# The last segment's projections are moved into attention's unit 0, between its score steps

## The chip, the cores and the metric

One NeuronCore of a Trainium2 chip runs the whole program. The engines are TensorE (PE; its weight loads are listed as PEld), VectorE (DVE), ScalarE (ACT), GpSimd (POOL) and SyncE (SP, whose queue issues most of the DMAs). The metric is the device time of one execution in microseconds (us), from the first to the last instruction and what lies around them. Less is better.

## The reference, cut to what matters

A transformer block: a layer norm modulated by a condition, attention over 2048 tokens in four segments of 512 with a memory that is carried from segment to segment, and a gated feed-forward layer. Width 576, 32 heads of 18, hidden width 4608, everything fp32.

```python
mod = (silu(c) @ w_mod).reshape(1, 6, 1, -1)
sa, ca, ga, sb, cb, gb = (mod[:, i] for i in range(6))
h = layernorm(x) * (1 + ca) + sa
q, k, v = h @ wq, h @ wk, h @ wv            # 32 heads x 18, 4 segments of 512
M, z = 0, 0
for s in range(4):
    p = softmax(q[s] @ k[s].T * scale + mask)
    a_dot = p @ v[s]
    a_mem = (phi(q[s]) @ M) / (phi(q[s]) @ z + 1e-6)      # phi(t) = t + 1 if t > 0 else exp(t)
    o[s] = g * a_mem + (1 - g) * a_dot
    M, z = M + phi(k[s]).T @ v[s], z + phi(k[s]).sum()
x = x + ga * (o @ wo)
h = layernorm(x) * (1 + cb) + sb
x = x + gb * ((silu(h @ w_gate) * (h @ w_up)) @ w_down)
```

## The kernel before

**Precision.** Matmuls take operands in the form float32r. To keep fp32 accuracy each operand is split into a high and a low part, and a product is made of three matmuls: high by high, high by low, low by high. The width 576 is four blocks of 128 and a rest of 64 (whose two parts share one tile, `hr`, so it needs two matmuls). One output tile of 128 rows by 512 tokens therefore takes 4 x 3 + 2 = 14 matmuls.

**Phase 1, projections.** The loop `for s in range(NSEG)` (L571) goes through the four segments. In this phase the Tile scheduler chooses the order on each engine by data, program order and its own costs. Per segment:

- nine projection tiles (`proj`, L505): five hold K, the last of them half, and the rest Q. Each takes the 14 matmuls of `mm14` (L100) into a PSUM tile `pp` (three buffers). ACT copies `pp` twice, to `fh` (the high part, L513) and `pf` (L514). DVE makes the low part `fl = pf - fh` (L515). SP stores both to DRAM (`kD`, `qD`), from where attention loads them as stacks. For Q rows of segments after the first, DVE makes `min(pf, 0)`, ACT its exponential and DVE `max(pf, 0)` plus that, which is phi(q) (`pq`, L529 to L531), and SP stores it (`qF`, L532).
- `phi_k` (L484 to L488): PE transposes a K tile to `ptk`, ACT and DVE make phi(k) of it (`pe`, `pk`). `ptk` has two buffers.
- four v pieces (`vproj`, `pv`, L545), the transposes of the next segment's input (`trans_in`, `pt`) and the memory update (`mem`, `pm`). Segment 3 has none of these: its v pieces are made in attention.

Two generators are stepped along with it. `early()` makes a part of the score passes of attention's first two units. `late_mod()` works off 20 pieces of `w_mod`: SP loads a piece (`wml`, four buffers, L430), DVE multiplies and adds it to `macc` (L349, L352), and after each fifth piece PE sums `macc` over partitions (`pc`, L359, L362) and DVE stores the sums (`colm`, L365, L366). It takes one step per projection tile from the middle of segment 1, and its last pieces fall into the v pieces of segment 2.

**Phase 2, attention.** From here the order is written by hand (`tc.manual_schedule()`), so each engine runs its instructions in the order of the code. A unit is four heads of one segment, so there are 32 units, eight per segment. Unit u does two passes of scores: the first pass of unit u+2 (matmuls of L184 into `s`, then DVE's custom instruction `junk`, `mx` of L199, which finds the row maxima) and the second pass of unit u (L656 into `s`, then ACT's exponential into `Pt`, L662). It multiplies `Pt` of unit u-1 by v (`av`, L679), transposes the result back (`px`, L700) and combines it. Units 0 to 7 also make the eight v pieces of segment 3 (`pw`, L803). Table `PAT` holds, for eleven slots of a unit, which of these events come in which order: an `a` is a pair of score steps, `M` and `X` are the parts of a v piece, `V` is `av`. Units 1 and 3 run the same row of `PAT`, and units 0 and 2 another.

**Loads of the units.** Four sets of stacks (`ks`, `qs`, for K and Q) are used in turn; `load_unit` (L168) has SP load a unit's four stacks from `kD` and `qD`. Those of units 0 to 2 are loaded in phase 1. Unit 3's set lies in the pool `sk2`, and its loads come first in phase 2, before unit 0. The loads of unit u+3 are issued at the start of unit u. Also ahead of unit 0, SP loads segment 0's v (`vq`, L724).

**Phase 3, feed-forward**, is set by PE and is not touched.

Of the kernel before, what the change touches and what calls it, by code (L numbers as in the profile page):

```python
# [11 lines left out]
ALU = mybir.AluOpType  # L12
# [52 lines left out]
LNA = 1  # L65
# [4 lines left out]
def f32(ap):  # L70
    return ap.bitcast(F32)
# [3 lines left out]
def block(ctx: ExitStack, tc: tile.TileContext, x, wqk, wv, wo, beta, wgu, wd, c, w_mod, wm01, out):  # L75
# [12 lines left out]
    def run(g):  # L88
        for _ in g:
            pass  # L90

    def mm14(ps, wh, wl, xh, xl, xr):
        k = 0
        for kt in range(5):
            if kt < 4:
                pairs = [(wh(kt), xh(kt)), (wl(kt), xh(kt)), (wh(kt), xl(kt))]
            else:
                pairs = [(wh(4), xr()), (wl(4), xr())]
            for a, b in pairs:
                nc.tensor.matmul(ps, lhsT=a, rhs=b, start=(k == 0), stop=(k == 13))  # L100
                k += 1

# [162 lines left out]

    p2, p2r, p7 = ExitStack(), ExitStack(), ExitStack()
    yx2 = pool(p7, "yx2", side="right")
# [5 lines left out]
    def v_ops(s, i, h):  # L273
# [6 lines left out]
        return ops + [(hr[:, tk], wvh[:, 4, sl]), (hr[:, tk], wvl[:, 4, sl])]  # L280

    with ExitStack() as p1:
        wq1 = pool(p1, "wq1")
        raw = pool(p1, "raw1", 2)
# [26 lines left out]

        wqkh = wq1.tile([P, 9, 5, P], F32R, tag="wqkh", name="wqkh")
        wqkl = wq1.tile([P, 9, 5, P], F32R, tag="wqkl", name="wqkl")
        bdm = w1.tile([P, 5, 8, VW], F32, tag="bdm", name="bdm")
# [190 lines left out]
        def proj(s, t):  # L505
            hh, hl, hr = hT[s]
            pp = ps.tile([P, L], F32, tag="p", name="pp", bufs=3)
            mm14(pp, lambda k: wqkh[:, t, k, :], lambda k: wqkl[:, t, k, :], lambda k: hh[k],
                 lambda k: hl[k], lambda: hr)
# [4 lines left out]
            nc.scalar.copy(f, pp)  # L514
            nc.vector.tensor_tensor(fl, f, f32(fh), op=ALU.subtract)  # L515
            k0, k1 = 128 * t, min(128 * t + 128, D)
            if k0 < D:
                n = k1 - k0
                nc.sync.dma_start(kD[s][k0:k1, 0:2, :], f32(fh[:n]).unsqueeze(1).to_broadcast([n, 2, L]))
                nc.sync.dma_start(kD[s][k0:k1, 2, :], f32(fl[:n]))  # L520
            q0, q1 = max(128 * t - D, 0), 128 * t + 128 - D
            if q1 > 0:
                n = q1 - q0
                r = P - n
                nc.sync.dma_start(qD[s][q0:q1, 0:3:2, :], f32(fh[r:]).unsqueeze(1).to_broadcast([n, 2, L]))
                nc.sync.dma_start(qD[s][q0:q1, 1, :], f32(fl[r:]))
                if s > 0:
                    e = pb.tile([P, L], F32, tag="pq1", name="pq1")
                    nc.vector.tensor_scalar(e[r:], f[r:], 0.0, None, op0=ALU.min)  # L529
                    nc.scalar.activation(e[r:], e[r:], AF.Exp)  # L530
                    nc.vector.scalar_tensor_tensor(e[r:], f[r:], 0.0, e[r:], op0=ALU.max, op1=ALU.add)  # L531
                    nc.sync.dma_start(qF[s][q0:q1, :], e[r:])  # L532
            return f
# [36 lines left out]

        for s in range(NSEG):  # L571
            gens = []
            if s == 0:
                gens.append(load_wv())
            if s + 1 < NSEG:
                gens.append(prep(s + 1))
            g = chain(*gens)
# [6 lines left out]
            for t in QKORD:  # L584
                if s == 0 and t + 3 < 9:
                    split_qk(t + 3)
                if s == 0 and t + 4 < 9:
                    load_qk(t + 4)
                f = proj(s, t)
                if pend is not None:  # L590
                    phi_k(s, *pend)
                    pend = None
                if t < 5 and s < 3:
# [9 lines left out]
            tg = trans_in(s + 1) if s + 1 < NSEG else iter(())  # L603
            for i in range(4):
                if i == 3:
                    for _ in g:
                        pass
                if s < 3:
                    vproj(s, i)
                next(g, None)  # L610
# [7 lines left out]
            next(tg, None)  # L618
            if s < 3:
                for _ in mem(s):  # L620
                    next(tg, None)
            for _ in tg:
# [7 lines left out]
    wk = pool(p2, "wk2", 2)  # L630
    opl_ = pool(p2, "op2")
    ps = pool(p2, "ps2", 2, space=PSUM)
# [92 lines left out]

    w3 = pool(p2r, "w3", side="right")
    o3 = pool(p2r, "o3", 2, side="right")
    yt = {}

    def yh(k, kb):  # L730
        return yt[1][:, k - 1, kb] if k else yt[0][kb]

    woh = w3.tile([P, 5, D], F32R, tag="woh", name="woh")
    wol = w3.tile([P, 5, D], F32R, tag="wol", name="wol")

# [50 lines left out]
    def wo_x(s, i, h):  # L786
# [3 lines left out]
        if h == 1:  # L790
            (nc.scalar if (s, i) == (2, 3) else nc.sync).dma_start(xD[s][:, i, :], xr)

    vst3 = {}
# [114 lines left out]
    def event(ev, u):  # L908
        n, a = ev[0], ev[1:]
        s, q = divmod(u, 8)  # L910
        if n == "V":
            for j in a:
# [11 lines left out]
        elif n == "d":  # L924
            comb_b(u - 1)
        elif n == "f" and s < 3 and q < 4:
            phi_q(s + 1, q + 1)
        elif n == "h" and s < 3 and q == 0:
            phi_q(s + 1, 0)
# [17 lines left out]
        elif n in "MX":  # L947
            w = u - 9
            if u < 8:
                if n == "M":  # L950
# [484 lines left out]
    with tc.manual_schedule():  # L1435
        new_stack(3, sk2)
        load_unit(3)
        for j in range(4):
            load_v(0, j)
        ot[0] = opl_.tile([P, 4, D], F32, tag="o0", name="o0")  # L1440
        for u in range(NU + 1):
            s, q = divmod(u, 8)
            if u:
                load_unit(u + 3)
            ma, mb = [], []
# [290 lines left out]
```

## Time and profile before

| what | us |
|---|---|
| three timed runs | 1858.72, 1859.91, 1860.71 (median 1859.91) |
| the profiled execution, its own time | 1856.97 |
| its span, first to last instruction | 1855.2 |
| segment 2: projections | 138.15 to 169.04 |
| segment 2: v pieces | 169.04 to 185.69 |
| transposes for segment 3 and memory update | 185.69 to 193.51 |
| segment 3: projections | 193.51 to 222.90 |
| unit 0 | 222.90 to 238.65 |
| unit 1 | 238.65 to 250.41 |
| unit 2 | 250.41 to 261.02 |
| unit 3 | 261.02 to 270.57 |

The stages are bounded by the first instruction on PE that belongs to the next one (in the last of the transposes, two matmuls of segment 3's first tile already stand between them). A row of the profile gives for one engine the start, the duration, the line, the operation with the tile that it writes and those that it reads, and in brackets how long the engine was idle before it and what ended that. In a table by windows, the columns are the length, the busy time of the five engines with the number of instructions, the clock that TensorE was granted as a share of full speed, the mean busy share of the DMA engines, and GB/s.

### The profile page before, as it was taken

The page shows a single profiled execution, that of the slowest core. Times are in us where ns is not written, and L with a number is a line of the kernel's source. Part 1 is how long each engine was busy: PE and PEld are TensorE (multiplying, and loading weights), DVE is VectorE, ACT ScalarE, POOL GpSimd, SP SyncE. Part 2 cuts the span into 40 slices and gives each one's busy share as a digit, 9 for nine tenths or more (in the row PEclk, how much of TensorE's full clock was granted, in tenths as well). Part 3 has the DMA queues.
Part 4 walks back from the last instruction along what each step waited for, and adds up shares of the span by engine and source line. Part 5 has one row for each costly group of instructions (what it writes and reads, how often), then busy time and mean ns, then how long its engine had stood idle before and what let it go on. Part 6 is the DMA issues. An engine that isn't in the chain of part 4 may idle for free.

```text
span 1855.2 us, 31128 instructions
## 1 busy us (share of the span) xinstructions
PE 1816.8 (98%) x11061; PEld 1518.0 (82%) x11061; DVE 1492.6 (80%) x3309; ACT 958.2 (52%) x2137; POOL 495.8 (27%) x702
## 2 busy tenths in 40 slices
PE   8999989999999999999999999999999999999999
PEld 5888756666667888888888888888888888888888
DVE  7566468888886888888888888758888888888887
ACT  6344457667776545445445444434454544544441
POOL 2010036454563345545544544300000000000000
PEclk9999999999999999999999999999999999999999
DMA  8677565558658654555555444395332333334331
GB/s 298 224 242 253 212 175 154 152 149 217 177 149 278 218 185 157 172 194 176 166 183 168 132 137 167 125 297 172 127 105 85 120 105 107 100 102 127 104 100 52
DMA packets 178562, 304.49 MB, mean 164 GB/s; under 512 B 25304, under 2 KB 108184, under 8 KB 176616
## 3 DMA queue, kind: packets, MB, share of 16 engines
q1 hardware_dynamic: 151032, 248.66, 42.7%
q10 hardware_dynamic: 27376, 53.86, 8.2%
q8 instruction: 87, 1.43, 0.3%
q14 instruction: 67, 0.55, 0.1%
HBM read 188.42 MB, written 113.33 MB: 163 GB/s over the span
## 4 chain that ended last, share of the span: by engine, by line
PE 87%; DVE 6%; DMA 4%; issue 1%; ACT 1%; SPq 1%; POOL 0%; ACTq 0%; DVEq 0%; POOLq 0%
PE A L1273 24%; PE pd L1401 13%; PE C L1273 12%; PE pd L1382 10%; PE B L1273 6%; PE pp L100 5%; PE av L679 3%; PE pw L784 3%; PE pv L545 2%; DVE junk L199 2%; PE s L184 2%; PE s L656 2%; DMA qs<-qD 1%; PE pn L862 1%; DMA y<-yD 1%
## 5 line engine op out<-in xcount | busy, mean ns | idle before, releaser
L1273 PE MATMUL A<-y,wh 128*128 128x512 f32 x1152 | 406.1, 393 | 1.1 <-ACT B L1319 0.7
L199 DVE CUSTOM_DVE_ANT_0 junk<-s,tri 128x384 bf16<-128x384 f32 (+3 forms) x512 | 222.0, 486 | 45.8 <-PE s L184 27.2
L1238 DVE TENSOR_TENSOR wl<-O,wh 128x256 fp32r<-128x256 f32 x504 | 253.7, 509 | 2.1 <-ACT wh L1237 1.6
L1273 PEld LDWEIGHTS A<-y,wh 128*128 128x128 f32 x1152 | 216.6, 188 | 45.9 <-ACT B L1319 2.2
L1273 PE MATMUL A<-y,wl 128*128 128x512 f32 x576 | 226.8, 394 | 0.0
L1387 DVE TENSOR_TENSOR acc<-acc,pd 128x576 f32<-128x576 f32 x216 | 162.3, 752 | 59.4 <-PE pd L1382 51.5
L1273 PE MATMUL C<-y,wh 128*128 128x512 f32 x576 | 202.9, 393 | 1.1 <-DVE cu L1296 1.1
L662 ACT ACTIVATE Pt<-s 128x512 f32<-128x512 f32 (+2 forms) x384 | 179.1, 525 | 44.7 <-PE s L184 24.4
L1237 ACT CAST wh<-O 128x256 fp32r<-128x256 f32 x504 | 197.5, 405 | 1.7 <-DMA yD<-st 0.8
L1401 PE MATMUL pd<-dh,ah 128*128 128x288 f32 x640 | 188.9, 295 | 0.5 <-DVE x L1405 0.5
L1401 PE MATMUL pd<-dh,al 128*128 128x288 f32 x640 | 189.0, 295 | 0.0
L1401 PE MATMUL pd<-dl,ah 128*128 128x288 f32 x640 | 188.7, 295 | 0.0
L1411 DVE TENSOR_TENSOR acc<-acc,pd 128x576 f32<-128x576 f32 x156 | 117.0, 750 | 87.9 <-PE pd L1401 87.2
L1228 POOL TENSOR_TENSOR O<-O 128x384 f32<-128x384 f32 x132 | 149.6, 1148 | 135.3 <-DMA O<-in_wgu_dram 61.5
L1342 ACT CAST ah<-sg 128x512 fp32r<-128x512 f32 x192 | 119.1, 621 | 77.2 <-DVE sg L1297 70.3
L1343 DVE TENSOR_TENSOR al<-sg,ah 128x512 fp32r<-128x512 f32 x192 | 136.3, 710 | 10.0 <-ACT ah L1342 9.9
L1382 PE MATMUL pd<-dh,ah 128*128 128x288 f32 x448 | 133.0, 297 | 0.0
L1382 PE MATMUL pd<-dh,al 128*128 128x288 f32 x448 | 132.5, 296 | 0.0
L1382 PE MATMUL pd<-dl,ah 128*128 128x288 f32 x448 | 132.3, 295 | 0.0
L184 PE MATMUL s<-ks,qs 54*128 54x512 f32 (+1 forms) x480 | 122.9, 360 | 8.2 <-DVE mx L199 4.2
L656 PE MATMUL s<-qs,ks 56*128 56x256 f32 (+3 forms) x512 | 124.5, 356 | 3.4 <-ACT Pt L662 2.8
L1401 PEld LDWEIGHTS pd<-dh,ah 128*128 128x128 f32 x640 | 120.7, 189 | 6.8 <-DVE x L1405 0.8
(388 smaller groups left out, 4337.2 us busy)
## 6 DMA issues: line engine op xcount, KB each, us to landing
O<-in_wgu_dram SPq DMA_DIRECT2D x36, 768.0 KB
O<-oD SPq DMA_DIRECT2D x36, 512.0 KB
oD<-O ACTq DMA_DIRECT2D x34, 512.0 KB
ks<-kD SPq DMA_DIRECT2D x64, 216.0 KB
qs<-qD SPq DMA_DIRECT2D x64, 216.0 KB
O<-in_wgu_dram SPq DMA_DIRECT2D x36, 384.0 KB
rD<-wr ACTq DMA_DIRECT2D x36, 336.0 KB
wr<-rD SPq DMA_DIRECT2D x35, 336.0 KB
```

The lines of the kernel that those rows point to most:

```text
L184: nc.tensor.matmul(bank[:, n * o:n * o + n], lhsT=qst[b][r, h // 2, 128 * i:128 * i + 128], rhs=kst[b][r, h // 2, 0:n], start=True, stop=True)
L199: nc.vector.tensor_tensor_reduce(junk[:, :n], bank[:, n * o:n * o + n], tri[:, L - n:], 1.0, -3e38, op0=ALU.add, op1=ALU.max, accum_out=mx ...
L656: nc.tensor.matmul(bank[:, n * o:n * o + n], lhsT=kst[u % NB][r, g // 2, 128 * j:128 * j + 128], rhs=qst[u % NB][r, g // 2, 128 * j:L], st ...
L662: nc.scalar.activation(pt[:, hs[0]:hs[-1] + 1:2, :n], bank[:, :n * per].rearrange("p (a b) -> p a b", a=per), AF.Exp, scale=SCALE)
L1228: eng.tensor_tensor(o[:, d], o[:, a], o[:, b], op=op)
L1237: nc.scalar.copy(wh, o)
L1238: later.append(lambda: nc.vector.tensor_tensor(wl, o, f32(wh), op=ALU.subtract))
L1273: nc.tensor.matmul(bank, lhsT=a, rhs=b, start=(first and n == 0), stop=(n == 6), skip_group_check=not first)
L1343: later.append(lambda: nc.vector.tensor_tensor(al, src, f32(ah), op=ALU.subtract))
L1382: nc.tensor.matmul(pd[:, i, :288], lhsT=a[:, tk], rhs=w, start=(k == 0), stop=(k == 2))
L1387: nc.vector.tensor_tensor(o, o, pd[:, :, :288], op=ALU.add)
L1401: nc.tensor.matmul(pd[:, i, :288], lhsT=a[:, tk], rhs=w, start=(k == 0), stop=(k == 5))
```

## The change

Attention's pools are opened right after segment 2, and phase 1's loop ends with it. Segment 3's nine projection tiles are nine events `W0` to `W8` of unit 0, four steps each, with three pairs of score steps after some of them; `W9` is the v piece that unit 0 had before. A tile's PSUM buffer is now one of the two of tag `x`. Its copies, low part and phi(q) go to two scratch tiles, `tmpa` and `tmpb`, in turn. They are not issued right behind the tile's matmuls: each further `W` step first advances the tiles before it by one part (low part and minimum; exponential and sum; stores). `late_mod` takes two steps per tile instead of one in the first five tiles of segment 2. Segment 0's v is loaded in slots 2 to 5 of unit 0. The weights' pool (`wqkh`, `wqkl`) lives on until the start of unit 1, and the pools of the output projection are opened there.

```diff
@@ PAT
+       ("W0 W0 W0 W0 a a a", "W1 W1 W1 W1 W2 W2 W2 W2 a a a", "W3 W3 W3 W3 W4 W4 W4 W4", "a a a", "W5 W5 W5 W5 W6 W6 W6 W6", "a a a", "W7 W7 W7 W7", "W8 W8 W8 W8", "W9 W9", "W9 W9", "P"))
@@ phase 1
-        for s in range(NSEG):
+        for s in range(3):
...
                 if s > 1 or s == 1 and t > 4:
                     next(gl, None)
+                if s > 1 and t < 5:
+                    next(gl, None)
@@ new, in attention
+    def seg3(t):
+        if not tmp3:
+            a = sk2.tile([P, 5, L], F32, tag="pq", name="tmpa").rearrange("p a b -> p (a b)")
+            b = vp.tile([P, 4, VC], F32, tag="vq", name="tmpb").rearrange("p a b -> p (a b)")
+            for v in (a, b):
+                tmp3.append([v[:, L * i:L * i + L] for i in range(4)])
+        f, fh, fl, e = tmp3[t % 2]
+        fh, fl = fh.bitcast(F32R), fl.bitcast(F32R)
+        pp = ps.tile([P, L], F32, tag="x", name="pp", bufs=XB)
+        ops = p_ops(3, t)
+        for c in range(WC):
+            for n in range(14 * c // WC, 14 * (c + 1) // WC):
+                nc.tensor.matmul(pp, lhsT=ops[n][0], rhs=ops[n][1], start=(n == 0), stop=(n == 13))
+            if c < 3:
+                yield
+        nc.scalar.copy(fh, pp)
+        nc.scalar.copy(f, pp)
+        yield
+        _, q1, r = q_rows(t)
+        nc.vector.tensor_tensor(fl, f, f32(fh), op=ALU.subtract)
+        if q1 > 0:
+            nc.vector.tensor_scalar(e[r:], f[r:], 0.0, None, op0=ALU.min)
+        yield
+        if q1 > 0:
+            nc.scalar.activation(e[r:], e[r:], AF.Exp)
+            nc.vector.scalar_tensor_tensor(e[r:], f[r:], 0.0, e[r:], op0=ALU.max, op1=ALU.add)
+        yield
+        k_store(3, t, fh, fl)
+        q_store(3, t, fh, fl)
...
+            nc.sync.dma_start(qF[3][q0:q1, :], e[r:])
+        yield
+    def seg3_step(t):
+        for g in list(s3q):
+            if next(g, 0) == 0:
+                s3q.remove(g)
...
+        if t == 9:
+            s3[9] = c = s3.get(9, -1) + 1
+            v_m(0, c)
+            if c == 3:
+                v_x(0)
+            return
+        if t not in s3:
+            s3[t] = [seg3(t), 0]
+        s3[t][1] += 1
+        next(s3[t][0])
+        if s3[t][1] == 4:
+            s3q.append(s3[t][0])
@@ phase 2
         load_unit(3)
-        for j in range(4):
-            load_v(0, j)
-        ot[0] = opl_.tile([P, 4, D], F32, tag="o0", name="o0")
...
+            if u == 1:
+                while s3q:
+                    seg3_step(-1)
+                p2q.close()
+                w3 = pool(p2r, "w3", side="right")
...
-                for ev in PAT[q // 4 * 2 + u % 2][k].split():
+                for ev in PAT[q // 4 * 2 + u % 2 if u else 4][k].split():
...
+                elif u == 0 and 2 <= k < 6:
+                    load_v(0, k - 2)
```

`p_ops`, `k_store`, `q_rows` and `q_store` hold what `proj` had in its own body. Two loads of `qF` that stood in units 0 and 1 now come together in unit 1.

PE, from the last matmuls of segment 3's projections into unit 0, before (`pp` is a projection tile, `s` a score tile; the line L656 is the second pass, L184 the first):

```order
L100 MATMUL pp<-hl_2191,wqkh 128x512
L100 MATMUL pp<-hr,wqkh 128x512
L100 MATMUL pp<-hr,wqkl 128x512
L656 MATMUL s_2602<-qs_982,ks_983 128x512
L184 MATMUL s_2605<-ks_991,qs_990 128x512
L184 MATMUL s_2612<-ks_991,qs_990 128x512
L656 MATMUL s_2611<-qs_982,ks_983 128x512
L656 MATMUL s_2618<-qs_982,ks_983 128x512
L184 MATMUL s_2619<-ks_991,qs_990 128x512
L184 MATMUL s_2626<-ks_991,qs_990 128x512
L656 MATMUL s_2625<-qs_982,ks_983 128x512
```

PE at the same place now, in unit 0 behind its first projection tile (L661 and L174 are the two passes, L807 the tile):

```order
L807 MATMUL pp<-hl_2197,wqkh 128x512
L807 MATMUL pp<-hr,wqkh 128x512
L807 MATMUL pp<-hr,wqkl 128x512
L661 MATMUL s_2369<-qs_982,ks_983 128x512
L174 MATMUL s_2372<-ks_991,qs_990 128x512
L174 MATMUL s_2379<-ks_991,qs_990 128x512
L661 MATMUL s_2378<-qs_982,ks_983 128x512
L661 MATMUL s_2385<-qs_982,ks_983 128x512
L174 MATMUL s_2386<-ks_991,qs_990 128x512
L807 MATMUL pp<-hh_2190,wqkh 128x512
L807 MATMUL pp<-hh_2190,wqkl 128x512
```

Before, all twelve pairs of score steps stood behind the ninth tile, with parts of the v piece between them from the seventh on. Now they go by threes, six matmuls or a few more at a time, behind the tiles 0, 2, 4 and 6.

DVE in the projections of segment 2, before, from the normalisation of the next segment's `x` on (`pe`, `pk` are phi(k), `pq` phi(q)):

```order
L249 TENSOR_SCALAR x_1743<-x_1743,mv,rs 128x576 x4
L488 SCALAR_TENSOR_TENSOR pk<-ptk,pe 128x4x128
L515 TENSOR_TENSOR fl<-pf,fh 128x512
L486 TENSOR_SCALAR pe<-ptk 128x512
L515 TENSOR_TENSOR fl<-pf,fh 128x512
L529 TENSOR_SCALAR pq_1900<-pf 64x512
L488 SCALAR_TENSOR_TENSOR pk<-ptk,pe 128x4x128
```

The same place now:

```order
L239 TENSOR_SCALAR x_1743<-x_1743,mv,rs 128x576 x4
L503 SCALAR_TENSOR_TENSOR pk<-ptk,pe 128x4x128
L380 TENSOR_SCALAR colm<-pc 128x2
L381 TENSOR_SCALAR colm<-pc 96x1
L380 TENSOR_SCALAR colm<-pc 128x2
L381 TENSOR_SCALAR colm<-pc 96x1
L364 TENSOR_SCALAR macc<-wml,sg 128x576
L529 TENSOR_TENSOR fl<-pf,fh 128x512
L501 TENSOR_SCALAR pe<-ptk 128x512
L367 SCALAR_TENSOR_TENSOR macc<-wml,sg,macc 128x576
L529 TENSOR_TENSOR fl<-pf,fh 128x512
L503 SCALAR_TENSOR_TENSOR pk<-ptk,pe 128x4x128
```

Four `colm` and two `macc` now stand between the two `pk`, and the minimum of the first `pq` has gone behind the second. On PE the `pc` matmuls that belong to these `colm` stand ahead of the third `ptk`; before they stood behind the fifth.

SP at the end of segment 3's stores, before:

```order
L525 DMA qD_90<-fh 128x2x512
L526 DMA qD_90<-fl 128x512
L532 DMA qF_98<-pq_2547 128x512
L125 DMA ks_2588<-ones 10x8x128
L125 DMA ks_2588<-ones 2x8x128
L168 DMA ks_2588<-kD_91 54x2x512
L168 DMA qs_2587<-qD_87 54x2x512
L168 DMA ks_2588<-kD_91 54x2x512
L168 DMA qs_2587<-qD_87 54x2x512
L724 DMA vq_2595<-vD_99 128x624 x4
```

SP now, at the end of segment 2's stores:

```order
L298 DMA qD_89<-fl 128x512
L539 DMA qF_97<-pq_2083 128x512
L115 DMA ks_2342<-ones 10x8x128
L115 DMA ks_2342<-ones 2x8x128
L158 DMA ks_2342<-kD_91 54x2x512
L158 DMA qs_2341<-qD_87 54x2x512
L158 DMA ks_2342<-kD_91 54x2x512
L158 DMA qs_2341<-qD_87 54x2x512
L287 DMA kD_94<-tmpa 128x2x512
L288 DMA kD_94<-tmpa 128x512
```

And at the end of segment 3's stores, where unit 1 begins:

```order
L297 DMA qD_90<-tmpa 128x2x512
L298 DMA qD_90<-tmpa 128x512
L826 DMA qF_98<-tmpa 128x512
L1033 DMA woraw<-in_wo_dram 128x576
L158 DMA ks_983<-kD_91 54x2x512
L158 DMA qs_982<-qD_87 54x2x512
L158 DMA ks_983<-kD_91 54x2x512
L158 DMA qs_982<-qD_87 54x2x512
```

The six loads of unit 3's stacks have gone from behind all of segment 3's stores to ahead of the first of them. Behind the last store now stand a piece of the output weights and the loads for unit 4. From unit 1 on, every engine runs the same instructions in the same order as before.

More of the change, by code (lines that the diff above doesn't have):

```diff
@@ L90, in run @@
             pass
[L92 to L101, printed above, removed]
     cst = pool(ctx, "cst")
@@ L280, in v_ops, with p_ops, k_store, q_rows @@
         return ops + [(hr[:, tk], wvh[:, 4, sl]), (hr[:, tk], wvl[:, 4, sl])]
+    wq1 = pool(p2q, "wq1", side="right")
+    wqkh = wq1.tile([P, 9, 5, P], F32R, tag="wqkh", name="wqkh")
+    wqkl = wq1.tile([P, 9, 5, P], F32R, tag="wqkl", name="wqkl")
+    def p_ops(s, t):
+        hh, hl, hr = hT[s]
+        ops = []
+        for k in range(4):
+            ops += [(wqkh[:, t, k, :], hh[k]), (wqkl[:, t, k, :], hh[k]), (wqkh[:, t, k, :], hl[k])]
+        return ops + [(wqkh[:, t, 4, :], hr), (wqkl[:, t, 4, :], hr)]
+    def k_store(s, t, fh, fl):
+        k0, k1 = 128 * t, min(128 * t + 128, D)
+        n = k1 - k0
+        if n > 0:
+            nc.sync.dma_start(kD[s][k0:k1, 0:2, :], f32(fh[:n]).unsqueeze(1).to_broadcast([n, 2, L]))
+            nc.sync.dma_start(kD[s][k0:k1, 2, :], f32(fl[:n]))
+    def q_rows(t):
+        q0, q1 = max(128 * t - D, 0), 128 * t + 128 - D
+        return q0, q1, P - (q1 - q0)
+    def q_store(s, t, fh, fl):
+        q0, q1, r = q_rows(t)
+        if q1 > 0:
+            nc.sync.dma_start(qD[s][q0:q1, 0:3:2, :], f32(fh[r:]).unsqueeze(1).to_broadcast([q1 - q0, 2, L]))
+            nc.sync.dma_start(qD[s][q0:q1, 1, :], f32(fl[r:]))
     with ExitStack() as p1:
-        wq1 = pool(p1, "wq1")
         raw = pool(p1, "raw1", 2)
@@ L505, in proj @@
         def proj(s, t):
-            hh, hl, hr = hT[s]
             pp = ps.tile([P, L], F32, tag="p", name="pp", bufs=3)
-            mm14(pp, lambda k: wqkh[:, t, k, :], lambda k: wqkl[:, t, k, :], lambda k: hh[k],
-                 lambda k: hl[k], lambda: hr)
+            for n, (a, b) in enumerate(p_ops(s, t)):
+                nc.tensor.matmul(pp, lhsT=a, rhs=b, start=(n == 0), stop=(n == 13))
             f = pb.tile([P, L], F32, tag="pf", name="pf")
@@ L515, in proj @@
             nc.vector.tensor_tensor(fl, f, f32(fh), op=ALU.subtract)
[L516 to L521, printed above, removed]
+            k_store(s, t, fh, fl)
+            q_store(s, t, fh, fl)
+            q0, q1, r = q_rows(t)
             if q1 > 0:
[L523 to L526, printed above, removed]
                 if s > 0:
@@ L592, in block @@
                     pend = None
-                if t < 5 and s < 3:
+                if t < 5:
                     pend = (t, f)
@@ L618, in block @@
             next(tg, None)
-            if s < 3:
-                for _ in mem(s):
-                    next(tg, None)
+            for _ in mem(s):
+                next(tg, None)
             for _ in tg:
@@ L948, in event @@
             w = u - 9
-            if u < 8:
+            if 0 < u < 8:
                 if n == "M":
```

40 lines of the change are left out of this document (24 added, 16 removed), and 2 rows, old and new, of the table PAT.

## The prediction
> **What bounds the kernel now.** I read the page first: the engines' shares and the chain that ended last.
>
> ```profile
> span 1855.2 us, 31128 instructions
> PE 1816.8 (98%) x11061; PEld 1518.0 (82%) x11061; DVE 1492.6 (80%) x3309; ACT 958.2 (52%) x2137; POOL 495.8 (27%) x702
> PE 87%; DVE 6%; DMA 4%; issue 1%; ACT 1%; SPq 1%; POOL 0%; ACTq 0%; DVEq 0%; POOLq 0%
> ```
>
> TensorE is busy for 98% of the span, so 38.4 us of it are idle in all. An edit that only moves matmuls can gain no more than such idle time, or matmuls that ran at a lower clock. So the next view is the table by stages (front table's bounds).
>
> ```profile
> 138.15:169.04 30.89, 29.45 (x151) 23.62 (x150) 24.40 (x53) 13.85 (x25) 1.83 (x2) 1.00 0.82 282
> 193.51:222.90 29.39, 29.39 (x126) 23.21 (x125) 10.67 (x18) 13.51 (x25) 0.00 (x0) 1.00 0.65 227
> 222.90:238.65 15.75, 9.99 (x48) 6.61 (x48) 8.84 (x36) 8.20 (x17) 3.72 (x10) 0.72 0.74 209
> 238.65:250.41 11.76, 11.51 (x83) 6.48 (x84) 6.29 (x25) 6.15 (x14) 2.90 (x6) 0.80 0.68 216
> 250.41:261.02 10.61, 9.60 (x85) 6.08 (x85) 9.33 (x40) 6.84 (x17) 4.25 (x10) 1.00 0.46 129
> 261.02:270.57 9.55, 9.30 (x84) 5.91 (x84) 6.79 (x32) 6.25 (x14) 2.92 (x9) 1.00 0.54 163
> ```
>
> Segment 3's projections are pure PE time, 29.39 of 29.39 at full clock. Unit 0 behind them is the worst stage here: 5.76 of 15.75 idle, and a clock of 0.72. Unit 1 hardly waits, but runs at 0.80. The waits of PE in unit 0, and then the chain there, say why:
>
> ```profile
> PE s L184 <- DMA qs<-qD: 3.3, 1, 3.3
> PE s L184 <- DVE mx L199: 2.0, 3, 0.9
> PE s L656 <- ACT pf L514: 0.5, 1, 0.5
> ```
>
> ```profile
> 227.08 0.32 SPq L532
> ...
> 229.22 0.42 SPq L168
> ...
> 230.46 8.05 DMA qs<-qD
> ...
> 238.65 0.89 PE s L184 x2
> ```
>
> Score steps alone outrun DVE (2.0). Then unit 0 has no more work, and unit 1's first pass waits 3.3 for unit 3's stacks, whose last load SP issues at 230.46, because it stands behind segment 3's last store (227.08). It takes 8.05 to land. The clock answers to this:
>
> ```profile
> 222.00:226.00 4.00, 2.52 (x13) 1.18 (x11) 2.49 (x6) 3.45 (x7) 0.00 (x0) 1.00 0.88 340
> 228.00:233.00 5.00, 5.00 (x20) 3.90 (x20) 2.28 (x10) 1.36 (x3) 0.30 (x1) 0.50 0.45 140
> 238.60:243.00 4.40, 4.35 (x23) 1.52 (x27) 1.31 (x4) 0.60 (x1) 0.00 (x0) 0.50 0.83 286
> 243.00:245.00 2.00, 2.00 (x24) 1.01 (x16) 0.38 (x1) 1.00 (x2) 1.32 (x1) 0.89 0.61 173
> 152.00:156.00 4.00, 2.56 (x14) 1.95 (x13) 3.94 (x9) 1.80 (x4) 0.00 (x0) 1.00 0.49 166
> ```
>
> After the thin stretch to 226 it is half, and after the wait to 238.65 it is half again until 243. In the last row a thin stretch that stayed at full clock.
>
> **The change, part by part.** All against the profiled execution, 1856.97 (the median of the runs is 2.94 above it).
>
> *Segment 2's projections.* `late_mod` brings DVE five `macc` earlier. Groups of DVE's instructions there, and PE's one stall:
>
> ```profile
> L352 DVE SCALAR_TENSOR_TENSOR macc<-wml,sg,macc 128x576 f32<-128x576 f32 (+1 forms) x11 | 8.9, 814 | 1.5 <-DMA wml<-in_w_mod_dram 1.4
> L515 DVE TENSOR_TENSOR fl<-pf,fh 128x512 fp32r<-128x512 f32 x9 | 6.2, 688 | 4.1 <-ACT pf L514 4.1
> 153.77 0.63 PE ptk L484 x4
> 154.40 3.03 PE pp L100 x13
> 157.42 0.39 PE ptk L484 x4
> 157.81 0.54 PE pc L359 x4
> ```
>
> ```profile
> 153.77 0.63 PE L484 MATMUL ptk<-ident,pf 128*128 128x128 f32 x4 [1.44 <-DVE pk L488]
> 159.15 0.50 PE L100 MATMUL pp<-hh,wqkh 128*128 128x512 f32 x1
> ```
>
> The `pc` matmuls for `colm` cost 159.15 - 157.81 = 1.34 there. They now come before the transpose that waits 1.44, so the 1.44 is filled: a gain of 1.34. But between the two `pk` that release the last two transposes now stand four `colm` and two `macc` (one of them the plain multiplication). Without them the second `pk` is in time, since the transpose at 157.42 does not wait. With them I work out 0.3 + 0.5 + 0.6 + 0.6 + 0.75 + 0.6 + 0.6 = 4.0 (a 688 ns instruction starts 0.60 after the one ahead) from the end of the first `pk`, 153.6, to 157.6, so PE may wait about 0.4 at 157.4. Net 0.9; I take 0.8. Bounds: +1.3 if it waits for nothing. On the other side, DVE has 24.40 of 30.89 busy; with 5 x 0.81 = 4.1 it has 28.5, so it fits, but its queue is in order, and a `macc` that waits for its `wml` holds `fl` and `pk` up. Two pieces per tile of 3.3 us with three loaded ahead leave a load 4.9 us. Its price when late is in these rows:
>
> ```profile
> 133.09 6.28 DMA wml<-in_w_mod_dram
> 148.62 2.67 DMA kD<-fl
> ```
>
> A landing of 2.67 is free. One of 6.28 costs 6.28 - 4.9 = 1.4 each time, and twice it would be a loss of 2.8 - 0.8 = 2.
>
> *Segment 3's projections.* The same 126 matmuls at 0.233, no gain. The two PSUM buffers (three before) are freed by ACT's two copies and the scratch by the stores. What could be late is costed under the second rival. At the seam the first tile no longer fills gaps among the last transposes: it stands behind them, and its thirteenth matmul needs `hr`, made from the last transpose by three instructions of ACT and DVE of about 0.7. Twelve matmuls (2.8) and the memory update cover these 2.1 with the handovers; the cost is nothing to 0.5, and I take 0.
>
> *Unit 0.* With tiles between the groups of scores, DVE and ACT get 3.3 to 6.5 us for the three pairs that PE gives out at a time, so the 2.0 of waits for `mx` go. The 0.5 for `pf` goes, as each tile has another behind it. Unit 3's loads are issued before the first store, some 35 us ahead of their use; the 3.3 goes. What stays is PE time at full clock. Unit 2 runs the same row of the table, with three groups in addition that unit 0 doesn't have:
>
> ```profile
> L679 PE MATMUL av<-Pt,vq 128*32 128x512 f32 (+3 forms) x32 | 2.4, 436 | 0.0
> L700 PE MATMUL px<-ident,avs 128*128 128x128 f32 x4 | 0.6, 272 | 0.0
> L214 PE MATMUL pmt<-ident,mc 128*32 128x128 f32 x1 | 0.3, 284 | 0.0
> ```
>
> 9.60 - 2.4 - 0.6 - 0.3 = 6.3. So 15.75 becomes 6.3: a gain of 9.45, the largest term.
>
> *Unit 1.* It now follows dense work. Unit 3 runs the same row of the table at clock 1.00 in 9.55, against 11.76: a gain of 2.2. The chain shows the same difference in `av`:
>
> ```profile
> 239.84 4.07 PE av L679 x32
> ...
> 262.01 2.29 PE av L679 x32
> ```
>
> [...]
>
> *What is late next.* The last tile's low part, minimum, exponential and sum fall into unit 0's v piece and the head of unit 1. The rows of the kernel before for such steps are 0.69, 0.42, 0.63, 0.69 in the order of a tile:
>
> ```profile
> 220.93 0.69 DVE L515 TENSOR_TENSOR fl<-pf,fh 128x512 fp32r<-128x512 f32 x1 [0.85 <-ACT pf L514]
> 222.00 0.63 ACT L530 ACTIVATE pq<-pq 128x512 f32<-128x512 f32 x1 [1.10 <-DVE pq L529]
> 222.66 0.69 DVE L531 SCALAR_TENSOR_TENSOR pq<-pf,pq 128x512 f32<-128x512 f32 x1 [0.70 <-ACT pq L530]
> ```
>
> Queued behind them are the first `junk` and `Pt` of unit 1, for which PE waits after three pairs; I take 1.0 (0 to 2). SP issues the last `qF` store only when that sum is there, some 2 to 3 us into unit 1, and the piece of output weights and unit 4's four loads stand behind it. They are needed at unit 2's start, 9.55 in; with 8.05 to land they come at 10 to 11. I take 0.5 (0 to 3).
>
> *Sum:* 0.8 + 9.45 + 2.2 - 1.5 = 10.95. The profiled execution would be 1846.0; the median 1859.91 - 10.95 = 1849.0.
>
> **The rivals.**
>
> *About half the gain is lost in unit 0.* Tile t's scratch is that of tile t+2. Copies 0.6 + 0.6, low part, minimum, exponential, sum and issue, each a step of a quarter tile behind, put the stores about 3 us behind the tile's end, and 2.67 to land makes 5.7; the copy of t+2 is due 6.5 after it (two tiles), 8 with a score group between. So there is 0.8 to 2.3 of room, and one more buffer of `pp` behind it. DMA speaks against it too: 0.65 busy in segment 3's projections with the same stores and PE dense. But loads of unit 3 and of v share the queue now. If the landing is 4 to 5, PE waits 1 to 1.5 at some four tiles: 5, and the median is 1854.
>
> *No change:* the gain is given back, because unit 2 waits for unit 4's stacks as unit 1 did for unit 3's (3.3), its clock falls again (2.2), and 3 to 5 go in unit 0: 1859. Against it: unit 4's loads have most of unit 1 in front of them.
>
> *Slower: the clock stays at half through unit 0.* Two PSUM buffers, each freed by ACT, and a score group that waits for DVE, give many small idle stretches. If they keep the clock at 0.50, the 35.7 us of PE work in unit 0 (29.4 + 6.3) take twice as long: +35.7 against the 9.45 + 2.2 gained, or 1884 when it is all of it; when it is two thirds, 1872. It decides from the point where busy falls below about 0.6 of a stretch of 4 us: 222 to 226 with 2.52 lost the clock, 152 to 156 with 2.56 did not. [...] The trace speaks against it here: segment 3's tiles run dense on three buffers with the same copies. A smaller kind of the same sign: stores that land in 6.28 hold every second tile for 3 or more.
>
> **How the numbers follow.** From no change, a measurement of this kernel tells about 0.2%, 3.7 us. The forecast has 0.68, half the gain 0.18, no change 0.06, slower 0.08. The likeliest gives 1849.0. Its own range is 1847 to 1852.5: with +1.3 in segment 2 and no tail the sum is 12.95, with the tail at 5 instead of 1.5 it is 7.45. The range over all takes in half the gain and leaves out the last two; at the fast side it goes 1.5 lower, since unit 2's 1.0 of idle time (10.61 - 9.60) may shrink too: 1845.5 to 1855. Faster by over 0.2% means below 1856.2: the forecast and half the gain, 0.86; within, 0.06; slower, 0.08.
>
> **What would show it.** Right: PE from the seam to unit 1 in one piece of about 36 us with a clock of 1.00 and no wait for `qs`; unit 1 at about 10.5 with `av` at 2.3; no wait at the third `ptk` and a small one at the last. Wrong: waits of `pp` for ACT's copy, and of that for a store (rival 1); a wait for `qs` or `ks` at unit 2's start; the clock below 1.00 within unit 0; `macc` waiting for `wml`, with `ptk` behind it. Any of the last two over 5 us would make the prediction wrong.

## The result, and the profile after

| | median us | runs | ratio to the kernel before, 95% interval |
|---|---|---|---|
| before | 1859.88 | 8 (1857.26 to 1860.71) | |
| changed | 1852.60 | 8 (1850.12 to 1858.02) | 0.9965 (0.9954 to 0.9975) |

The change makes the kernel faster by a little: 0.35% of 1859.9 is 6.5 us, with the interval 4.6 to 8.6 (the ratio is that of the means; the two medians are 7.3 apart). The forecast was 10.9. The direction and the range held; the size was too large by 4.4.

The profiled execution of the changed kernel took 1858.02. It is the slowest of the eight, while that of the kernel before (1856.97) was faster than each of its eight timed runs. So the two spans must not be subtracted. The stages can be compared, and a second profile of the changed kernel (`again`, 1854.66) stands beside the first.

The shares on the page after are those of before:

```profile
span 1856.1 us, 31118 instructions
PE 1817.6 (98%) x11061; PEld 1519.7 (82%) x11061; DVE 1492.4 (80%) x3309; ACT 955.5 (51%) x2137; POOL 495.2 (27%) x702
```

The table by stages of the changed kernel, with the columns of before: unit 0 with its nine projection tiles, unit 1, unit 2, unit 3.

```profile
195.80:230.64 34.84, 34.84 (x172) 27.62 (x172) 18.13 (x49) 16.31 (x33) 4.75 (x10) 1.00 0.66 218
230.64:245.14 14.50, 9.94 (x84) 6.20 (x84) 10.43 (x39) 8.58 (x20) 5.48 (x11) 0.94 0.89 257
245.14:257.67 12.53, 11.65 (x84) 6.84 (x85) 6.94 (x28) 6.47 (x15) 2.01 (x5) 0.79 0.44 130
257.67:267.24 9.57, 9.32 (x83) 5.92 (x84) 6.79 (x32) 6.25 (x14) 2.91 (x9) 1.00 0.51 159
```

Unit 0 is what was forecast: PE busy for all of 34.84 us, at clock 1.00. Unit 1 is not: 14.50 against 11.76 before, though nearly all its PE work ran at full clock. Unit 2 takes 12.53 against 10.61, at clock 0.79. Unit 3 is as before. PE's rows show where the time of unit 1 goes, and the chain of waits what it is:

```profile
240.87 0.27 PE L661 MATMUL s<-qs,ks 56*128 56x128 f32 x1
245.14 0.76 PE L661 MATMUL s<-qs,ks 56*128 56x512 f32 x1 [4.00 <-DMA qs<-mr]
245.52 0.89 PE L174 MATMUL s<-ks,qs 54*128 54x512 f32 x2
...
247.06 3.96 PE L684 MATMUL av<-Pt,vq 128*32 128x512 f32 x32
```

```profile
236.63 8.37 DMA qs<-mr
```

Unit 2's second pass needs the row maxima that its first pass found in unit 0. They are transposed (`pmt`), copied (`mr`) and sent by DMA into two rows of the stack `qs`. These two DMAs of 8 KB had landed 8.37 us after the first of them was issued. PE waited 4.00, its clock fell (to 0.50 at 243.5, within the wait), and `av` of unit 1 took 3.96 instead of the 2.36 that the next one takes at clock 1.00, in unit 3. SP's queue shows what stands ahead of them (start, time of issue, DMA):

```profile
234.06 0.32 SPq L826 DMA_DIRECT2D qF<-tmpa  x1
234.43 0.52 SPq L1033 DMA_DIRECT2D woraw<-in_wo_dram  x1
235.04 0.34 SPq L158 DMA_DIRECT2D ks<-kD  x1
...
236.20 0.34 SPq L158 DMA_DIRECT2D qs<-qD  x1
236.63 1.44 SPq L163 DMA_DIRECT2D qs<-mr  x2
238.12 2.40 SPq L907 DMA_DIRECT2D pq<-qF  x3
```

The last tile's last store goes out at 234.06, 3.4 us into unit 1. Behind it come the piece of output weights, unit 4's four loads (864 KB), the row maxima, and three loads of phi(q). The DMA engines were already full, as windows of 4 us from the second half of unit 0 into unit 1 show (their busy share is the number before the last):

```profile
222.00:226.00 4.00, 4.00 (x23) 3.27 (x22) 3.30 (x15) 2.50 (x7) 2.53 (x7) 1.00 1.01 320
226.00:230.00 4.00, 4.00 (x23) 3.53 (x22) 2.24 (x4) 1.49 (x3) 0.00 (x0) 1.00 0.95 340
230.00:234.00 4.00, 3.71 (x43) 1.93 (x41) 1.69 (x4) 2.40 (x6) 0.00 (x0) 1.00 1.05 404
```

The other loss is ahead of unit 0. A part of it is in segment 2's projections:

```profile
148.92 0.60 PE L374 MATMUL pc<-ones,macc 128*128 128x1 f32 x4 [0.83 <-DVE macc L367]
...
150.32 0.66 PE L499 MATMUL ptk<-ident,pf 128*128 128x128 f32 x4
```

```profile
148.00:152.00 4.00, 3.17 (x29) 2.80 (x29) 3.46 (x9) 1.69 (x3) 1.02 (x1) 0.92 1.04 382
152.00:156.00 4.00, 4.00 (x14) 3.11 (x13) 4.00 (x11) 0.14 (x1) 0.00 (x0) 0.65 0.66 243
```

The `pc` matmuls, which the prediction put into a stall, wait 0.83 themselves; and the clock falls behind them (0.65 from 152 to 156), so that 14 matmuls fill 4 us in which 17 would fit at full speed (0.233 each). Another part lies at the seam between the last v piece and unit 0; it is counted below.

### The profile page after: what moved, and what is told of

Its sections match the earlier page's. It is cut to its first block, busy times and chain, and to the rows that moved or that the text cites. A ratio compares the mean times of both kernels' runs of the same rounds, so it can differ in the third digit from the quotient of the medians.

```text
span 1856.1 us, 31118 instructions
## 1 busy us (share of the span) xinstructions
PE 1817.6 (98%) x11061; PEld 1519.7 (82%) x11061; DVE 1492.4 (80%) x3309; ACT 955.5 (51%) x2137; POOL 495.2 (27%) x702
## 4 chain that ended last, share of the span: by engine, by line
PE 87%; DVE 6%; DMA 3%; issue 2%; ACT 1%; POOL 0%; SPq 0%; ACTq 0%; DVEq 0%; POOLq 0%
PE A L1335 24%; PE pd L1463 13%; PE C L1335 12%; PE pd L1444 10%; PE B L1335 6%; PE av L684 4%; PE pp L523 3%; PE pw L784 3%; PE pv L552 2%; PE s L661 2%; PE s L174 2%; DVE junk L189 2%; PE pp L807 2%; DMA qs<-mr 1%; DMA y<-yD 1%
## 5 line engine op out<-in xcount | busy, mean ns | idle before, releaser
L1300 DVE TENSOR_TENSOR wl<-O,wh 128x256 fp32r<-128x256 f32 x504 | 249.4, 500 | 2.1 <-ACT wh L1299 1.6
L1404 ACT CAST ah<-sg 128x512 fp32r<-128x512 f32 x192 | 119.1, 621 | 77.5 <-DVE sg L1359 69.9
L661 PE MATMUL s<-qs,ks 56*128 56x256 f32 (+3 forms) x512 | 124.0, 356 | 8.2 <-DMA qs<-mr 5.4
L1463 PEld LDWEIGHTS pd<-dl,ah 128*128 128x128 f32 x640 | 120.6, 188 | 7.1
```

The lines of the kernel that those rows point to most:

```text
L661: nc.tensor.matmul(bank[:, n * o:n * o + n], lhsT=kst[u % NB][r, g // 2, 128 * j:128 * j + 128], rhs=qst[u % NB][r, g // 2, 128 * j:L], st ...
L1300: later.append(lambda: nc.vector.tensor_tensor(wl, o, f32(wh), op=ALU.subtract))
L1404: nc.scalar.copy(ah, src)
L1463: nc.tensor.matmul(pd[:, i, :288], lhsT=a[:, tk], rhs=w, start=(k == 0), stop=(k == 5))
```

## The experiments

Theory A: the forecast gain is made in unit 0 and part of it is lost again at unit 2, because loads that stand behind the last tile's stores (unit 4's stacks ahead of all) keep the row maxima back; a smaller part is lost in segment 2, where the generator's steps come too early. The rivals: the three phi(q) loads crowd the row maxima (B), or all of it is chance (C). Each ratio below is against runs of the kernel before on the same chip.

**The same kernel again (`again`, `again2`).** No edit.

> The changed kernel once more, to see what of its first profile recurs. That execution took 1858.02, the longest of the eight, and its clock record has five half-clock windows of about 3.4 us: one in segment 2's projections (near 151), two at unit 2, one near unit 6 (301), one in the feed-forward (574). Theory A: the late start of unit 2 (4.0 us of waiting for the row maxima qs<-mr, then two half-clock windows) belongs to the kernel and recurs within 1.5 us; the windows at 301 and 574 do not, and the profiled execution takes 1851 to 1854. Rival C: the wait at unit 2 is chance as well and is gone or under 1 us, and the execution takes about 1848 to 1850. The pc wait for macc in segment 2 (0.8 to 1.0) recurs under both.

> The changed kernel a third time, on the same chip as best2, for the direct comparison. The wait for the row maxima at unit 2 (3.8 to 4.0 in two profiles) and two half-clock windows behind it recur; the window near 151 (one of two profiles) does not need to. 1852 to 1854.

Medians 1854.14 (ratio 0.9973, 0.9961 to 0.9986) and 1854.09 (0.9969, 0.9957 to 0.9980). With the eight runs of the result the median is 1853.5 (24 runs). The stages of `again`, in the order of above:

```profile
194.57:229.44 34.87, 34.87 (x172) 27.59 (x172) 18.13 (x49) 16.30 (x33) 4.75 (x10) 1.00 0.66 217
229.44:243.71 14.27, 9.93 (x84) 6.19 (x84) 10.39 (x39) 8.59 (x20) 5.47 (x11) 0.97 0.89 261
243.71:256.50 12.79, 11.91 (x85) 6.92 (x85) 6.94 (x28) 6.47 (x15) 2.01 (x5) 0.77 0.43 130
```

The wait for the row maxima recurs (3.77 here, 3.7 in `again2`), and so does the half clock in unit 2. It belongs to the kernel; C falls for this part. The clock's fall in segment 2 does not recur: it was chance, and with it about 1 us of the first profile (unit 0 begins at 194.57 here, at 195.80 there). The wait of the `pc` ahead of it recurs at half its length (0.5 and 0.4).

**The kernel before again (`before_again`).** No edit.

> The kernel before once more, for the half-clock windows. Its first profile has two of 6.8 us at units 0 and 1 and none where attention ends (near 575); the changed kernel and its variants have one of 3.4 us there in four of five profiles. If that window belongs to the change, it is absent here again; if it is chance of when a window of the clock's record begins, it may well stand here too. The two at units 0 and 1 recur under both.

1860.13. The stretches of half clock that the traces record, in whole us of the span (the one at the very end left out):

```
before         226 (6.8 us)   237 (6.8)
before_again   228 (3.4)      235 (10.2)   263 (3.4)
changed        151 (3.4)      244 (6.8)    302 (3.4)   575 (3.4)
again          243 (6.8)      570 (3.4)
again2         241 (6.8)      572 (3.4)
late_q         241 (6.8)
load4_early    241 (6.8)      569 (3.4)
pq_later       240 (6.8)      568 (3.4)
load4_wo       252 (3.4)
vq_wo          242 (3.4)
best           249 (3.4)      420 (3.4)    566 (3.4)
best2          none
```

Half clock at units 0 and 1 recurs in the kernel before, 13.7 us of it in both profiles; the second has a stretch of 3.4 at 263 on top. At the start of unit 4 the second is 2.7 us later than the first (273.25 and 270.57). So the execution against which the prediction made its sum had lost less there than the other one. Where attention ends (566 to 575) there is none in two profiles of the kernel before, but one in six of the ten of the changed kernel and its variants, which run the same work there. Two profiles don't tell whether that belongs to the change; it stays open.

**The generator's steps in the Q tiles (`late_q`).**

```diff
-                if s > 1 and t < 5:
+                if s > 1 and t > 3:
                     next(gl, None)
```

> The five extra steps of the w_mod generator are taken in the tiles 4 to 8 of segment 2 (Q) instead of 0 to 4 (K); all else as changed. Theory A: in the changed kernel the column sums pc come ahead of the third ptk and wait 0.83 for macc, PE then runs 1.4 us of very small matmuls, and half clock follows (8 matmuls at 0.43 instead of 0.235: 1.6). With the steps later the pc wait and the half clock go; the ptk wait of the kernel before (1.44) may come back. So 0.5 to 2.5 faster than the changed kernel: 1850 to 1852. Rival: DVE's load in the K tiles is not what costs, only the half-clock window is, and it comes by chance; then within 0.7 of the changed kernel, 1852.6.

1852.86 (0.9964, 0.9951 to 0.9977), which cannot be told from the changed kernel; by the time alone the rival's figure came. In the profile the effect is there. The `pc` stand ahead of the next `ptk` and nothing waits:

```profile
151.62 0.50 PE L374 MATMUL pc<-ones,macc 128*128 128x1 f32 x4
...
153.27 0.63 PE L499 MATMUL ptk<-ident,pf 128*128 128x128 f32 x4
```

Unit 0's first tile begins at 192.95, against 195.80, 194.57 and 193.96 in the three profiles of the changed kernel: 1.0 to 2.8 earlier. The stage is better as expected; in the time it cannot be seen beside the spread of the runs (1851.5 to 1856.7 in `again`).

**Unit 4's loads earlier (`load4_early`).**

```diff
-            if u:
+            if u > 1:
                 load_unit(u + 3)
...
+                elif u == 0 and k == 6:
+                    load_unit(4)
```

> Unit 4's four stack loads are issued in unit 0 behind tile 6's stores, ahead of those of tiles 7 and 8, instead of at unit 1's start behind all of them. Theory A: the row maxima of unit 2 land late because 864 KB of unit 4's stacks stand just ahead of them in the DMA queues. Then qs<-mr lands 2 to 4 us earlier, the 4.0 wait falls to 0 to 1.5 and the clock does not fall in unit 2: 3 to 5 us faster than the changed kernel, 1848 to 1850. Rival B (the three phi(q) loads issued right behind the maxima share the DMA engines with them): the wait stays above 3 us and the time within 1 us of 1852.6.

1852.81 (0.9963, 0.9953 to 0.9973): no gain. But the wait is another one. PE's row at unit 2's start and POOL's row of the output weights:

```profile
242.95 0.79 PE L661 MATMUL s<-qs,ks 56*128 56x512 f32 x1 [3.85 <-ACT Pt L667]
```

```profile
240.30 1.40 POOL L1037 TENSOR_TENSOR woraw<-woraw,gaB 128x576 f32<-128x576 f32 x1 [16.77 <-DMA woraw<-in_wo_dram]
```

The row maxima are no longer what comes last. ACT's copy of the output weights stands ahead of unit 1's last exponentials in ACT's queue, it needs POOL's scaling, and that waits for a load that was issued at 233.38 behind the last stores and landed 6.9 us later. One late load took the place of the other. The time was a miss; that loads behind the last stores are the cause is tried next.

**The phi(q) loads later (`pq_later`).**

```diff
-            if u == 1:
+            if u == 2:
                 phi_q(1, 0)
                 phi_q(1, 1)
-            phi_q(s + 1, q + 1)
+                phi_q(1, 2)
+            if u == 3:
+                phi_q(1, 3)
+            if u > 2:
+                phi_q(s + 1, q + 1)
```

> The three phi(q) loads that the change put together into unit 1 (640 KB, issued right behind unit 2's row maxima) are issued one unit later; the fourth one unit later too. Rival B: qs<-mr lands 2 us or more earlier and unit 2's wait of 4.0 falls below 2: 3 to 5 us faster, 1848 to 1850. Theory A: they stand behind the maxima in the same queue, so the landing changes by less than 1 us and the time stays within 1 us of 1852.6.

1852.15 (0.9963, 0.9947 to 0.9978). The landing of the row maxima, from the chains of `again` and then of `pq_later`, and PE's row in the latter:

```profile
235.41 8.17 DMA qs<-mr
```

```profile
234.56 6.49 DMA qs<-mr
```

```profile
241.19 0.76 PE L661 MATMUL s<-qs,ks 56*128 56x512 f32 x1 [2.17 <-DMA qs<-mr]
```

It lands 1.7 sooner and PE waits 2.2 instead of 3.8. That lies between the two expectations, while the time is the changed kernel's. In the four profiles with the three loads behind them the row maxima landed after 8.4, 8.2, 8.1 (`again2`) and 7.9 (`late_q`). So loads issued behind them seem to slow them: B holds a part, and theory A in its strict form (what is behind does not matter) was wrong, as far as one profile without the loads can tell.

**Both late loads ahead of the stores (`load4_wo`).** `load4_early`, and:

```diff
-       ("W0 W0 W0 W0 a a a", ...
+       ("P W0 W0 W0 W0 a a a", ...
-        ... "W9 W9", "W9 W9", "P"))
+        ... "W9 W9", "W9 W9", ""))
```

> As load4_early, and the piece of output weights (woraw, 288 KB) is loaded at the start of unit 0 instead of behind the last tile's stores. In load4_early the wait for the row maxima was gone, but unit 2's first score step waited 3.85 for ACT, whose copy of that piece waited for POOL and POOL for the load (landed 6.9 after its issue). Theory A': the loads behind the last stores are the cost, one behind the other; with both ahead of them unit 2's wait falls to 0 to 1, its clock stays at 1.00, av of unit 2 comes 11 to 12 after unit 1's, and the time is 3 to 5 us under the changed kernel: 1848 to 1850. Rival: a third thing is late there (wait still over 2, half clock in unit 2) and the time is 1852 to 1853.

1850.57 (0.9949, 0.9931 to 0.9967). Unit 2 starts at 239.52 without a wait and at full clock, 4.2 earlier than in `again` (0.5 of it was there at unit 0's start). So issuing both loads earlier, with the same bytes, removes this wait (3.77 in `again`, 3.85 for ACT in `load4_early`). Then unit 3 waits:

```profile
251.63 0.70 PE L661 MATMUL s<-qs,ks 56*128 56x512 f32 x1 [1.75 <-DMA qs<-mr]
```

Its row maxima stand behind unit 5's loads in the same queue; one half-clock stretch of 3.4 us goes with it. The time lies just above the 1848 to 1850 that were expected, and its interval overlaps those of the changed kernel, so a gain over it shows in the profile only.

**Fewer bytes late in unit 0 (`vq_wo`).** The changed kernel with `P` moved as above, and:

```diff
         load_unit(3)
+        for j in range(4):
+            load_v(0, j)
...
-                elif u == 0 and 2 <= k < 6:
-                    load_v(0, k - 2)
```

> Only bytes are taken out of the stretch from 213 to 238 in which the DMA engines are 0.95 to 1.05 busy: segment 0's v (1.25 MB) is loaded ahead of unit 0 as in the kernel before, and the output weights' piece at unit 0's start; unit 4's loads stay behind the last stores. Theory A' (order in the queue): the row maxima still stand behind unit 4's 864 KB, so a wait of 1.5 to 3 stays and the clock falls in unit 2; 0 to 2 us under the changed kernel. Rival (the amount of bytes): 1.5 MB less at some 400 GB/s is 3.8 us less backlog, so the wait is gone and the time 3 to 5 under it.

1849.26 (0.9949, 0.9934 to 0.9964).

```profile
242.15 0.47 PE L661 MATMUL s<-qs,ks 56*128 56x512 f32 x1 [2.68 <-DMA qs<-mr]
```

The wait is 2.7 instead of 3.8, as the order theory expected (1.5 to 3), and not gone, as the amount of bytes alone would have it. The time speaks for the rival: it is 3.3 under the 1852.6 of the changed kernel, where the order theory had 0 to 2 and the rival 3 to 5 (four runs, and the intervals of the two kernels overlap). From the start of unit 0 to `av` of unit 4 the profile has 69.9, and `again` 73.0: 1.1 less of waiting, half clock for 3.4 instead of 6.8 us, and unit 1's last score step ends 9.5 after the unit's start, not 10.5. The last 1.0 goes with a wait that the changed kernel has and this one lacks: that of the last tile's copies for the scratch. In the changed kernel:

```profile
ACT tmpa L810 <- DMA qD<-tmpa: 1.9, 1, 1.9
```

This wait of ACT for tile 6's stores is in `again` too (1.9), and it is gone in `vq_wo` and in the combined version. Without it the copies come 1.3 earlier against unit 1's start, and so does the last store (2.1 behind that start, not 3.4), with all that stands behind it in SP's queue.

**All of it (`best`, `best2`).** `late_q`, `load4_wo`, `vq_wo` and `pq_later` together.

> All of it together: extra steps of the w_mod generator in tiles 4 to 8, unit 4's loads ahead of the last two tiles' stores, v and the output weights' piece ahead of unit 0, phi(q) one unit later. Theory A': no wait over 1 us at unit 2, no half clock from unit 0 to unit 3, no wait of pc in segment 2: unit 3's av 9 to 11 us earlier than in the kernel before (4.5 in the changed one), and the time 1847.5 to 1850. Rival: the gain at unit 3 is paid later (unit 4 or where attention ends), and the time stays at 1851 to 1853.

> The combined version again. If the queue of loads at unit 1 is what kept the gain from the forecast, no wait over 1 us at unit 2 recurs, unit 3's av stands 10 to 12 earlier than in the first profile of the kernel before, and the time is 4 to 8 us under that of again2. The half-clock windows of the first profile at 420 and 566 do not belong to it and need not recur. Rival: the first result was chance, and it lies within 3 us of again2.

1846.66 (0.9934, 0.9919 to 0.9949) and 1845.32 (0.9920, 0.9904 to 0.9937); the intervals of `best2` and `again2`, measured side by side, do not overlap. In neither does unit 2 or unit 3 wait for the row maxima. One expectation failed: `best` has a half-clock stretch of 3.4 us at the start of unit 3 (249), though the only wait in the 10 us ahead of it is one that `best2` has too, without such a stretch:

```profile
247.69 0.32 PE L174 MATMUL s<-ks,qs 54*128 54x128 f32 x1 [0.88 <-DVE mx L189]
```

The stages of `best2`:

```profile
192.99:227.86 34.87, 34.87 (x173) 27.63 (x173) 19.20 (x50) 17.15 (x34) 6.69 (x11) 1.00 0.73 239
227.86:237.39 9.53, 9.28 (x85) 5.92 (x85) 7.62 (x28) 7.46 (x17) 1.45 (x5) 1.00 0.83 272
237.39:247.99 10.60, 9.61 (x84) 6.05 (x84) 9.32 (x40) 6.84 (x17) 4.24 (x10) 1.00 0.58 168
247.99:257.56 9.57, 9.32 (x84) 5.93 (x84) 6.79 (x32) 6.25 (x14) 3.44 (x10) 1.00 0.54 164
```

Unit 1 takes 9.53, unit 2 10.60, unit 3 9.57, all at clock 1.00: the lengths that the prediction had for them, without the 1.0 that it added to unit 1. Unit 3 starts 13.0 earlier than in the first profile of the kernel before. This version beats both kernels: 8.8 us under the changed one (1845.3 against 1854.1 on one chip), a little more than the 4 to 8 expected.

## Why the prediction was right, and where its size came from

- **Segment 2, +0.8 forecast (bounds -2 to +1.3): +0.9, +1.0 and, with the half clock, -1.0.** From the first `ptk` to the end of the last v piece PE does the same work in both kernels but for one transpose. The kernel before takes 44.9 from 140.82 on, `again` 43.9 from 141.31, `again2` 43.9 and the first profile 45.9. "The 1.44 is filled" held, since no `ptk` waits any more; but the `pc` stand on PE one `ptk` earlier than that stall and wait for `macc` themselves (0.4 to 0.8). `late_q`, where they don't, takes 42.9. The stall of the last `ptk`, for which 0.4 was put, did not come. In `before_again` the stall to be filled was only 0.93 (44.3 in all), so this gain depends on the execution too.
- **The seam, taken at 0 (nothing to 0.5): -1.9, the first step that failed.** From the last v piece to segment 3's first tile the kernel before has the equal of 7.4 on PE: 185.69 to 193.51, less 1.4 for the tile matmuls begun by then (the trace has five, not the two named with the stages), and 1.0 more for four sums of `macc` that now come ahead. The changed kernel takes 9.3 in all three profiles. Of the 1.9, 0.8 are waits:

```profile
189.70 1.11 PE L512 MATMUL pm<-vs,pk 128*128 128x76 f32 x8 [0.16 <-ACT gbB L387]
...
191.15 1.30 PE L512 MATMUL pm<-vs,pk 128*128 128x152 f32 x8 [0.22 <-DVE mbd L515]
...
194.57 0.50 PE L807 MATMUL pp<-hh,wqkh 128*128 128x512 f32 x1 [0.41 <-DVE mbd L515]
```

The rest, about 1.1, is in the transposes and the memory update, which take longer without an idle entry where no tile's matmuls stand between them; what lengthens them is not shown.

- **Unit 0, +9.45: right, and a little low.** No score step and no tile behind the first waited, and the clock stayed at 1.00. The rival of half clock through unit 0 is refuted by these windows. PE work of 35.7 us was forecast, and unit 0 took 34.84 to 34.87. Counted from the same point (193.1 in the kernel before), the stage was 45.55, so the gain is 10.7. The 29.4 put for the tiles holds the four sums (1.0) and lacks the five matmuls (1.4); the score steps and the v piece were over-sized, with about 5.1 (34.85 less 29.8) in place of 6.3.
- **Unit 1 at full clock, +2.2, and 1.0 back for DVE and ACT: right, the 1.0 in part by luck.** Its last score step ends at 241.1 in the changed kernel, 10.5 after the start, and 9.55 + 1.0 was forecast. But the last tile's steps cost this only in the profiles in which ACT's copies had waited for the scratch, a wait that the term does not have; where they come 1.3 sooner (`vq_wo`, `best2`), unit 1 takes 9.5.
- **What is late next, 0.5 (0 to 3): the step that failed most.** The prediction named SP's queue, the last `qF` store and unit 4's loads behind it, and asked when unit 4's stacks are needed. It did not ask for the row maxima that stand behind these loads in the same queue and are needed at the same time. It measured 3.7 to 4.0 of waiting and 1.9 to 2.2 of half clock in unit 2, 6 in place of 0.5. `load4_wo` and `best2` show that it is this queue: with unit 4's loads and the output weights ahead of the stores unit 2's wait and half clock are gone, and with the other loads moved too, so is unit 3's wait.
- **The rivals.** The one called "no change" had this mechanism nearly to the price (3.3 and 2.2, for unit 4's stacks), but it was thought to need a loss in unit 0 as well, and was given 0.06. The one on scratch had its place right and its victim wrong: PE never waited for a tile's copy, but ACT did once, by 1.9, which made the loads of unit 1 1.3 later. The rival of half clock put the point where the clock falls at about 0.6 of a stretch of 4 us; in the changed kernel it fell with 3.17 of 4 busy (148 to 152), so that point does not hold.
- **The base.** The sum was made against an execution with little half clock in units 0 to 2; `before_again` is 2.7 later at the start of unit 4. Against that one `again` gains 7.2 there, against the first profile 4.5; the 6.5 of the timed runs lie between.

## What to carry to other kernels

When a stage is made dense, what was issued in its idle time is issued later or in a shorter time (here the last store went from 11.6 us ahead of unit 1's start to 3.4 behind it): follow each DMA queue over the seam and list everything behind the last store, the small transfers too, with the time at which each is needed. Removing one late load may show the next (3.85 of waiting for ACT in `load4_early`, 1.75 at unit 3 in `load4_wo`); move them together before the idea is judged. And compare several profiles before two spans are subtracted: a stage without half clock can be read from one (unit 3 took 9.55 to 9.57 in four), a sum of 10 us in 1850 cannot.

## What the hardware did that was not expected

The clock's stretches of half speed last 3.4, 6.8 or 10.2 us in all profiles (but for the one at the very end), multiples of one length. The waits that went with them differ: 4.00 us in the changed kernel (unit 2), 1.75 in `load4_wo` (unit 3), and 0.83 with 1.4 us of small matmuls behind it in the changed kernel (segment 2); waits of 0.5 and 0.4 at that last place (`again`, `again2`) went with none. The length of the wait does not decide alone. In `vq_wo` the wait at that place was 1.29, and the clock stayed:

```profile
149.83 0.61 PE L374 MATMUL pc<-ones,macc 128*128 128x1 f32 x4 [1.29 <-DVE macc L367]
```

In `best` the clock fell behind a wait of 0.88 and in `best2` it did not, with 3.12 of 4 us of PE busy ahead of it in both (245 to 249). The same instructions at the end of attention had a half-clock stretch in some executions and none in others. What decides is open. In the stretch in segment 2 of the changed kernel the matmuls start 0.43 us apart (151.63 to 154.62) instead of 0.233, so its 3.4 us cost about 1.6 (an estimate: 3.4 less 3.4 x 0.233 / 0.43). The changed kernel's eight runs spread over 7.9 us, more than the change is worth; their mean granted clocks run from 0.995 in the slowest to 0.998 in the fastest, and 0.003 of 1853 is 5.6 us.

Two DMAs of 8 KB took 7.9 to 8.4 us to land behind 864 KB and ahead of 640 KB of other loads (four profiles), and 6.5 when the latter were not there (one profile). So the loads issued behind them may have delayed them. If only what stood ahead had counted, those loads would not have mattered; with one profile without them, this stays open.
